# Batch 7's k and v loads, v casts and k exponential at other places of a hand-ordered attention-then-MLP kernel

## The chip, the core and the metric

The kernel runs on one core of a Trainium2 chip. The time is that of one execution on the device in microseconds (us). Before the change it is 277.86 us, the median of three runs (277.82 to 278.19).

## The reference

Attention without a score matrix, for 8 batches of 8 heads, 576 positions and 64 columns, and behind it two matrix products:

```python
def _attn_ref(q, k, v):
    q_s = np.exp(q - np.max(q, axis=-1, keepdims=True))
    q_s = q_s / (np.sum(q_s, axis=-1, keepdims=True) + 1e-09)
    k_s = np.exp(k - np.max(k, axis=2, keepdims=True))
    k_s = k_s / (np.sum(k_s, axis=2, keepdims=True) + 1e-09)
    kv = np.einsum('bhsd,bhse->bhde', k_s, v)
    return np.einsum('bhsd,bhde->bhse', q_s, kv)

def _moe_ref(x, w_in, w_out):
    h = x @ w_in
    return np.maximum(0.01 * h, h) @ w_out
```

q is normalized over its 64 columns, k over the 576 positions. The result, with batch and position joined to 4608 tokens of 512 columns, is x; `w_in` is 512x2048 and `w_out` 2048x512.

## The kernel before

The 4608 tokens are worked through in 9 tiles of 512, counted from 0. A tile has 64 matmuls of layer 1 (16 blocks j of hidden columns, 4 matmuls each, line L563), whose sums ScalarE passes through the leaky activation (`leaky`, L572), and then layer 2 (L584): four sub-blocks of 128 tokens, each of 16 matmuls into one PSUM buffer `pout`. Tiles 3 and 4, of which the change speaks, both go so. At the end of a sub-block ScalarE copies `pout` to `out_sb` (`store`, L578) and SyncE issues two stores of 128 KB (L581). There are two `pout` buffers for layer 2, so sub-block 3 writes into the one that sub-block 1's copy has to have read; there are four `out_sb`.

The attention of later batches runs beside that. For one batch the steps are:

- `load_all` (L84): SyncE loads k, q and v into buffers of a pool of six (`raw_pool`). A buffer comes free when the last reader of its old tile is done. Batch 7's k takes the place of batch 5's v, batch 7's v that of batch 5's k, and batch 7's q that of batch 5's q.
- k: VectorE takes the maximum over positions (`k_max`, that is `k_tree`, L160), carries it across partitions and subtracts it (`k_less`, that is `k_allmax` and `k_sub`, L167 to L198); ScalarE takes the exponential (`k_exp`, L206).
- v: two casts to bf16 into `vb2` (`v_cast`, L216), on ScalarE for batches 5 to 7 (`casts_act`).
- q: maximum and difference on VectorE (`q_front`, L245 and L304), the exponential on ScalarE (`q_exp`, L312), sum, reciprocal and product on VectorE (`q_ready`, L321, L323 and L328), and a transposing DMA that SyncE issues (`q_turn`, L551).
- `attend_kv(b)`: on TensorE, the k-v product of batch b+1 (L341, into `pokv`) interleaved with the product of batch b's q and its k-v matrix (L479); on VectorE the scaling of the new k-v matrix (`kd_make`, L361 and L362); on ScalarE six copies into `xT`, the input of layer 1 (`x_keep`, L500).

The order is written out by hand. `at(t, u, ...)` hangs steps on a place of tile t: u from 0 to 15 is behind layer 1's block u, u = 16+4s+m behind the 4(m+1)-th matmul of sub-block s. The steps of a place are recorded when TensorE's program gets there, and each engine then takes its own instructions in that order, without overtaking. So a step moved by `at` moves on every engine that it uses, SyncE's queue of DMA issues among them, and an instruction that waits holds up all behind it on its engine. Every DMA of SyncE takes the next of eight semaphores in turn and first waits until the DMA that had that semaphore before has landed.

Two steps behind these matter as well. At (5, 12), `in_weight_sums` gives GpSimd eight sums and differences of `w_in` halves (L824). It takes inputs that were there long before, and writes into `t`, whose buffer is that of batch 7's v: GpSimd, which has nothing ahead of it, starts when batch 7's v casts have read that buffer. And at (5, 0) and (5, 9) batch 7's q exponential and its transpose follow.

Of the kernel before, what the change touches and what calls it, by code (L numbers as in the profile page):

```python
# [26 lines left out]
def kernel(  # L27
# [50 lines left out]
    def load(src, b, name, cuts, t=None):  # L78
        t = raw(name) if t is None else t
        flat = src[b].rearrange("h s d -> (h s d)").rearrange(  # L80
            "(hl p r d) -> p hl r d", hl=HL, p=P, r=R
        )
        for hs, rs in cuts:
            nc.sync.dma_start(  # L84
                out=t[:, hs, rs].rearrange("p h r d -> p h (r d)"),
                in_=flat[:, hs, rs].rearrange("p h r d -> p h (r d)"),
            )
        return t

    ALLH, ALLR = slice(0, HL), slice(0, R)  # L90
# [114 lines left out]
    def k_exp(b, hs):  # L205
        nc.scalar.activation(  # L206
            out=st[b]["ke"][:, :, hs].rearrange("p r h d -> p h r d"),
            in_=st[b]["k"][:, hs],
            func=AF.Exp,
        )  # L210

    def v_cast(eng, b, gg):
        o = vb2[b % 2][:, :, gg, :, 0:D].rearrange("p r h d -> p h r d")
        i = st[b]["v"][:, 2 * gg : 2 * gg + 2]
        if eng is nc.scalar:
            eng.copy(out=o, in_=i)  # L216
        else:
            eng.tensor_copy(out=o, in_=i)  # L218
# [10 lines left out]
    def turned(name):  # L229
        return qT_pool.tile([P, XE.stop, P], BF16, name=name, tag="qT")  # L230
# [87 lines left out]
    def q_sum(b, rs, hs=ALLH):  # L318
        n, m = rs.stop - rs.start, hs.stop - hs.start
        qsum = small_pool.tile([P, n, HL], FP32, name="qsum")[:, :, 0:m]  # L320
        nc.vector.reduce_sum(out=qsum, in_=q_cols(b, rs, hs), axis=AX.X)  # L321
        st[b]["qrec", rs.start, hs.start] = qrec = small_pool.tile([P, n, HL], FP32, name="qrec")[:, :, 0:m]
        nc.vector.reciprocal(out=qrec, in_=qsum)  # L323

    def q_norm(b, rs, hs=ALLH, out=None):
        n, m = rs.stop - rs.start, hs.stop - hs.start
        qes = q_cols(b, rs, hs)
        nc.vector.tensor_tensor(  # L328
            out=qes if out is None else out,
            in0=qes,  # L330
            in1=st[b]["qrec", rs.start, hs.start].unsqueeze(3).to_broadcast([P, n, m, D]),
            op=ALU.mult,
        )


    def kv_quads(b, gg, outs, rs=ALLR):
        for r in range(R)[rs]:
            for hp in range(2):
                for hh in range(2):
                    rows = slice(hh * L, (hh + 1) * L)  # L340
                    nc.tensor.matmul(  # L341
                        outs[hh][hp * D : (hp + 1) * D, 0 : D + 1],
                        lhsT=st[b]["ke"][rows, r, 2 * gg + hp],
                        rhs=vb2[b % 2][rows, r, gg, hp, 0 : D + 1],
                        start=(r == 0),
                        stop=(r == R - 1),
                    )
# [9 lines left out]
    def kd_make(b):  # L357
        for hh in range(2):
            pkv = st[b]["pkv"][hh]
            krec = small_pool.tile([P, 2, 1], FP32, name="krec")  # L360
            nc.vector.reciprocal(out=krec, in_=pkv[:, :, D : D + 1])  # L361
            nc.vector.tensor_tensor(  # L362
                out=kd2[b % 2][:, :, hh],
                in0=pkv[:, :, 0:D],
                in1=krec.to_broadcast([P, 2, D]),
                op=ALU.mult,
            )
# [96 lines left out]
    def cross(b, gg, outs, rows):  # L464
        for hp in range(2):
            for hh in range(2):
                half = slice(hp * D, (hp + 1) * D)
                ls = slice(hh * L, (hh + 1) * L)
                if b == 0 and rows.start == R3.start:
                    rhs = st[1]["X1"][:, X8][:, gg : gg + 1, ls]  # L470
                elif b == 1 and rows.start == RE.start:
                    rhs = st[1]["X1"][:, XE].rearrange("c (r g) l -> c g r l", g=2)[:, gg, :, ls]
                elif b == 1:
                    rhs = st[1]["X1"][:, XH[gg], ls]
                elif "qX" in st[b]:
                    rhs = st[b]["qX"].rearrange("c (r g) (h l) -> c g h r l", g=2, h=2)[:, gg, hh, rows]
                else:
                    rhs = st[b]["qT"][:, 2 * hh + gg, rows]
                nc.tensor.matmul(  # L479
                    outs[hp][hh * D : (hh + 1) * D].rearrange("p (r l) -> p r l", l=L),  # L480
                    lhsT=kd0[half, gg, hh, hp] if b == 0 else kd2[b % 2][half, gg, hh],
                    rhs=rhs[half],
                    start=True,
                    stop=True,
                )

    def attend(b, ggs, rows, pool=psB_pool, tag=BANK_TAG):
        n = (rows.stop - rows.start) * L
        ps = [pool.tile([P, len(ggs), n], FP32, name="po", tag=tag) for _ in range(2)]
        for i, gg in enumerate(ggs):  # L490
            cross(b, gg, [ps[hp][:, i] for hp in range(2)], rows)
        st[b]["po", ggs, rows.start] = ps

    def x_keep(eng, b, ggs, rows, hp):
        ps = st[b]["po", ggs, rows.start][hp]
        c0, c1 = b * S + rows.start * L, b * S + rows.stop * L
        s0 = 2 * ggs[0] + hp
        o = xT[:, s0 : 2 * ggs[-1] + hp + 1 : 2, c0:c1]
        if eng is nc.scalar:
            eng.copy(out=o, in_=ps)  # L500
        else:
            eng.tensor_copy(out=o, in_=ps)

    def attend_kv(b, rows=R7, rest=RE):
        n = 2 * (rest.stop - rest.start) * L
        both = [psB_pool.tile([P, n + 2 * (D + 2)], FP32, name="pokv", tag=BANK_TAG) for _ in range(2)]
        ps = [a[:, 0:n].rearrange("p (g c) -> p g c", g=2) for a in both]
        st[b + 1]["pkv"] = pkv = [a[:, n:].rearrange("p (g d) -> p g d", g=2) for a in both]
        part = lambda gg, r0, r1: kv_quads(b + 1, gg, [pkv[hh][:, gg] for hh in range(2)], slice(r0, r1))
        part(0, 0, 6)  # L510
        attend(b, (0,), rows)
        part(0, 6, R)
        part(1, 0, 3)
        attend(b, (1,), rows)
        part(1, 3, R)
        for gg in range(2):
            cross(b, gg, [ps[hp][:, gg] for hp in range(2)], rest)
        keep = [lambda gg=gg, hp=hp: x_keep(nc.scalar, b, (gg,), rows, hp) for gg in range(2) for hp in range(2)]
        st[b]["po", (0, 1), rest.start] = ps
        kd_make(b + 1)  # L520
        for fn in keep:
            fn()
        for hp in range(2):
            x_keep(nc.scalar, b, (0, 1), rest, hp)
# [23 lines left out]
    def q_turn(b, rs=ALLR):  # L548
        if rs.start == 0:
            st[b]["qX"] = turned("qX")[:, 0 : 2 * R]  # L550
        nc.sync.dma_start_transpose(  # L551
            out=st[b]["qX"][:, 2 * rs.start : 2 * rs.stop],
            in_=st[b]["qe"][:, rs].rearrange("p r h d -> p (r h d)"),
        )
# [40 lines left out]
    def at(t, u, *fns):  # L595
        while t > 0 and u >= 32:
            t, u = t + 1, u - 32
        hooks.setdefault((t, u), []).extend(fns)
# [7 lines left out]
    def load_all(b, order="kqv"):  # L606
        for name in order:
            cuts = [(H0, ALLR), (H1, ALLR)] if b == B - 1 or (b, name) in ((B - 2, "q"), (B - 2, "v")) else [(ALLH, ALLR)]
            st[b][name] = load(dict(q=q, k=k, v=v)[name], b, f"{name}_raw", cuts)
# [155 lines left out]
    def k_max(b, t, u):  # L765
        at(t, u, lambda: k_begin(b), lambda: q_begin(b), lambda: k_tree(b, ALLH))

    def k_less(b, t, u):
        at(t, u, lambda: k_allmax(b), lambda: k_sub(nc.vector, b, ALLH))

    def q_ready(b, t, u):
        at(t, u, lambda: q_sum(b, ALLR), lambda: q_norm(b, ALLR))

    def casts_act(b, *slots):
        for gg, (t, u) in enumerate(slots):
            at(t, u, lambda gg=gg: v_cast(nc.scalar, b, gg))
# [12 lines left out]
    at(3, 20, lambda: q_exp(5, ALLR))  # L789
    q_ready(5, 3, 20)  # L790
    casts_act(6, (3, 28), (3, 30))
    at(3, 31, lambda: q_turn(5), lambda: load_all(7, "kvq"))
    k_less(6, 3, 31)
    at(4, 4, lambda: k_exp(6, ALLH))
    q_front(6, 4, 4)
    at(4, 9, lambda: q_exp(6, ALLR))
    k_max(7, 4, 9)
    q_ready(6, 4, 9)
    at(4, 17, lambda: attend_kv(5))
    k_less(7, 4, 18)  # L800
    at(4, 20, lambda: q_turn(6))
    casts_act(7, (4, 20), (4, 22))
    at(4, 24, lambda: k_exp(7, ALLH))
    q_front(7, 4, 24)
    at(4, 28, lambda: attend_kv(6))
    at(5, 0, lambda: q_exp(7, ALLR))
# [712 lines left out]
```

## Time and profile before

| what | value |
|---|---|
| median of three runs | 277.86 us (277.82 to 278.19) |
| the profiled execution, its own time | 277.69 us |
| span of its instructions | 275.7 us |
| TensorE, busy | 269.0 us, 98% |
| VectorE, busy | 225.9 us, 82% |
| ScalarE, busy | 184.9 us, 67% |
| GpSimd, busy | 81.8 us, 30% |
| tile 3, layer 1 and layer 2 | about 105.5 to 119.2 and 119.2 to 134.3 us |
| tile 4, layer 1 and layer 2 | about 134.3 to 148.1 and 148.1 to 165.3 us |

All times inside the program are counted from the span's start. In the profile's lines PE is TensorE, PEld its weight loads, DVE VectorE, ACT ScalarE, POOL GpSimd, and SPq SyncE's queue of DMA issues. `ke<-k_raw` means that `ke` is written and `k_raw` read. In a timeline a line has the start, the length, the engine, the code line, the operation, the tiles and how many instructions it merges; `[0.75 <-ACT ke L206]` says that the engine stood idle for 0.75 us ahead of it, and what ended that.

### The profile page before, as it was taken

How to read it: one execution, taken by the hardware profiler on the slowest of the kernel's cores; microseconds unless marked ns; L12 is line 12 of the kernel's file. 1: busy time of each engine (PE TensorE's matmuls, PEld its weight loads, DVE VectorE, ACT ScalarE, POOL GpSimd, SP SyncE). 2: the span in 40 equal slices, each digit the busy share in tenths (PEclk: the TensorE clock that was granted, in tenths of full speed). 3: DMA queues.
4: the chain of work that ended last, by engine and by line, in shares of the span. 5: the costliest groups of instructions: out<-in, count | busy, mean ns of one | idle time of the engine just before them, and what ended most of it. 6: DMA issues, size and time to landing. Idle time of an engine off the chain costs nothing.

```text
span 275.7 us, 5464 instructions
## 1 busy us (share of the span) xinstructions
PE 269.0 (98%) x2114; PEld 162.9 (59%) x2114; DVE 225.9 (82%) x330; ACT 184.9 (67%) x336; POOL 81.8 (30%) x97
## 2 busy tenths in 40 slices
PE   8899999999999999999999989999999999999994
PEld 3478644444444454454444444466776777889994
DVE  2996995899999999978978998979954756669962
ACT  4977573784489368985797669657746767984241
POOL 2866460149003000000000194000001999950000
PEclk9999999999999999999999999999999999999999
DMA  7999999987997699696398271400033000015254
GB/s 246 332 209 322 242 267 262 391 272 238 251 386 259 70 348 333 110 390 186 83 268 326 56 148 38 86 4 0 2 76 76 0 4 0 0 36 131 66 115 115
DMA packets 40569, 46.48 MB, mean 169 GB/s; under 512 B 18912, under 2 KB 24288, under 8 KB 40544
## 3 DMA queue, kind: packets, MB, share of 16 engines
q1 hardware_dynamic: 36720, 41.56, 51.3%
q0 software_dynamic: 3504, 4.20, 8.7%
q10 hardware_dynamic: 320, 0.39, 0.4%
q8 instruction: 16, 0.26, 0.4%
q14 instruction: 9, 0.07, 0.1%
HBM read 36.70 MB, written 9.44 MB: 167 GB/s over the span
## 4 chain that ended last, share of the span: by engine, by line
PE 85%; DVE 8%; DMA 4%; ACT 1%; SPq 1%; issue 0%; DVEq 0%
PE ph L563 32%; PE pout L584 21%; PE pout L1094 10%; PE pq L1343 10%; PE pp L1062 9%; DMA k_raw<-in_k_dram 4%; DVE t L160 2%; PE po L479 1%; ACT ke L206 1%; DVE k_raw L198 1%; DVE qe L328 1%; DVE qsum L321 1%; PE pkv L341 1%; PE pokv L341 1%; PE pkv L419 0%; DVE k_raw L410 0%
## 5 line engine op out<-in xcount | busy, mean ns | idle before, releaser
L563 PE MATMUL ph<-xT,w_in_sb 128*128 128x512 bf16 (+1 forms) x512 | 99.5, 353 | 0.0
L563 PEld LDWEIGHTS <-w_in_sb 128*128 128x128 bf16 x512 | 49.4, 98 | 46.0 <-issue 0.2
L584 PE MATMUL pout<-w_out_sb,gj 128*128 128x512 bf16 x320 | 71.4, 379 | 0.0
L572 ACT ACTIVATE gj<-ph 128x512 bf16<-128x512 f32 x88 | 49.1, 605 | 13.7 <-PE ph L563 13.1
L584 PEld LDWEIGHTS <-gj 128*128 128x128 bf16 x320 | 30.6, 98 | 36.1 <-issue 0.2
L824 POOL TENSOR_TENSOR t<-w_in_sb 128x256 fp32r<-128x256 bf16 x16 | 12.3, 772 | 68.7 <-DMA out_dram<-out_sb 68.7
L328 DVE TENSOR_TENSOR qe<-qe,qrec 128x2304 bf16<-128x2304 bf16 (+5 forms) x13 | 21.5, 1657 | 0.4
L321 DVE TENSOR_REDUCE qsum<-qe 128x36 f32<-128x2304 bf16 (+5 forms) x13 | 20.1, 1542 | 2.2 <-ACT qe L312 2.0
L206 ACT ACTIVATE ke<-k_raw 128x2304 bf16<-128x2304 f32 (+2 forms) x13 | 18.0, 1383 | 4.2 <-DVE k_raw L198 3.7
L578 ACT COPY out_sb<-pout 128x512 f32<-128x512 f32 x16 | 9.4, 589 | 16.5 <-PE pout L584 13.4
L245 DVE TENSOR_REDUCE qmax<-q_raw 128x36 f32<-128x2304 f32 (+5 forms) x13 | 20.0, 1537 | 0.5 <-DMA q_raw<-in_q_dram 0.5
L312 ACT ACTIVATE qe<-q_raw 128x2304 bf16<-128x2304 f32 (+5 forms) x13 | 17.3, 1328 | 4.2 <-POOL q_raw L304 3.2
L198 DVE TENSOR_TENSOR k_raw<-k_raw,kall 128x1152 f32<-128x1152 f32 (+2 forms) x10 | 18.1, 1821 | 0.3
L572 ACT ACTIVATE xT<-ph 128x512 bf16<-128x512 f32 x24 | 13.9, 605 | 5.9 <-PE ph L563 5.8
L304 POOL TENSOR_TENSOR q_raw<-q_raw,qmax 128x512 f32<-128x512 f32 (+3 forms) x7 | 11.8, 1681 | 20.4 <-DVE qmax L245 20.0
L1259 DVE COPY u<-pp 128x512 f32<-128x512 f32 x8 | 5.5, 692 | 13.6 <-PE pp L1062 13.6
L500 ACT CAST xT<-po 128x448 bf16<-128x448 f32 (+3 forms) x31 | 13.2, 509 | 4.4 <-PE po L479 4.4
L824 POOL TENSOR_TENSOR t<-w_in_sb,t 128x256 fp32r<-128x256 bf16 x16 | 15.1, 943 | 0.6
L218 POOL CAST vb<-v_raw 128x1152 bf16<-128x1152 f32 x7 | 9.8, 1436 | 17.1 <-DMA v_raw<-in_v_dram 17.1
L304 DVE TENSOR_TENSOR q_raw<-q_raw,qmax 128x2304 f32<-128x2304 f32 (+1 forms) x6 | 13.7, 2290 | 0.2
L1062 PE MATMUL pp<-s,t 128*128 128x512 f32 x48 | 13.9, 398 | 0.0
L160 DVE TENSOR_TENSOR t<-k_raw 128x512 f32<-128x512 f32 (+1 forms) x11 | 10.2, 930 | 3.7 <-DMA k_raw<-in_k_dram 3.6
(169 smaller groups left out, 434.0 us busy)
## 6 DMA issues: line engine op xcount, KB each, us to landing
out_dram<-out_sb SPq DMA_DIRECT2D x60, 128.0 KB, 2.5
k_raw<-in_k_dram SPq DMA_DIRECT2D x8, 576.0 KB, 5.8
v_raw<-in_v_dram SPq DMA_DIRECT2D x8, 576.0 KB, 7.4
q_raw<-in_q_dram SPq DMA_DIRECT2D x4, 1152.0 KB, 9.4
v_raw<-in_v_dram SPq DMA_DIRECT2D x4, 1152.0 KB, 11.6
k_raw<-in_k_dram SPq DMA_DIRECT2D x4, 1152.0 KB, 6.3
q_raw<-in_q_dram SPq DMA_DIRECT2D x4, 576.0 KB, 8.5
w_in_sb<-in_moe_w_in_dram POOLq DMA_DIRECT2D x7, 256.0 KB, 6.9
```

The source lines that it names most:

```text
L198: eng.tensor_tensor(out=ks, in0=ks, in1=st[b]["kall"][:, hs].unsqueeze(2).to_broadcast([P, n, R, D]), op=ALU.subtract,)
L206: nc.scalar.activation(out=st[b]["ke"][:, :, hs].rearrange("p r h d -> p h r d"), in_=st[b]["k"][:, hs], func=AF.Exp,)
L304: eng.tensor_tensor(out=qs, in0=qs, in1=st[b]["qmax", rs.start, hs.start].unsqueeze(3).to_broadcast([P, m, n, D]), op=ALU.subtract,)
L321: nc.vector.reduce_sum(out=qsum, in_=q_cols(b, rs, hs), axis=AX.X)
L328: nc.vector.tensor_tensor(out=qes if out is None else out, in0=qes, in1=st[b]["qrec", rs.start, hs.start].unsqueeze(3).to_broadcast([P, n, ...
L563: nc.tensor.matmul(ph, lhsT=w_in_sb[:, cb, j * P : (j + 1) * P], rhs=xT[:, cb, c0 : c0 + n], start=(cb == 0 and first), stop=(cb == NB - 1 ...
L572: nc.scalar.activation(out=o, in_=ph, func=AF.Prelu, alpha=LEAKY_SLOPE)
L584: nc.tensor.matmul(pout, lhsT=g_sb[j // 2][:, j % 2, tsub * P : (tsub + 1) * P], rhs=w_out_sb[:, j, os], start=(j == 0), stop=(j == NF - 1),)
L824: eng.tensor_tensor(out=late[o], in0=a, in1=b, op=ALU.subtract)
L1062: nc.tensor.matmul(ps, lhsT=w(c), rhs=a(c), start=(first and c == 0), stop=(c == 1), skip_group_check=True)
L1094: nc.tensor.matmul(ps[:, i], lhsT=a(m)[:, i * P : (i + 1) * P], rhs=w(m), start=(first and m == 0 and i == 0), stop=(m == NH - 1 and i == ...
L1343: nc.tensor.matmul(ps[i], lhsT=a(m)[:, i * P : (i + 1) * P], rhs=w(m), start=(first and m == 0 and (each or i == 0)), stop=(m == NH - 1 an ...
```

## The change

```diff
     q_ready(5, 3, 20)
     casts_act(6, (3, 28), (3, 30))
-    at(3, 31, lambda: q_turn(5), lambda: load_all(7, "kvq"))
+    at(3, 22, lambda: load_all(7, "kv"))
+    at(3, 31, lambda: q_turn(5), lambda: load_all(7, "q"))
     k_less(6, 3, 31)
...
     q_ready(6, 4, 9)
+    casts_act(7, (4, 16), (4, 16))
     at(4, 17, lambda: attend_kv(5))
     k_less(7, 4, 18)
-    at(4, 20, lambda: q_turn(6))
-    casts_act(7, (4, 20), (4, 22))
-    at(4, 24, lambda: k_exp(7, ALLH))
+    at(4, 18, lambda: q_turn(6))
+    at(4, 22, lambda: k_exp(7, ALLH))
     q_front(7, 4, 24)
```

Four steps move: batch 7's k and v loads from the end of tile 3 to its sub-block 1, batch 7's v casts from sub-block 1 of tile 4 to the start of its sub-block 0, batch 6's q transpose from sub-block 1 to sub-block 0, and batch 7's k exponential from sub-block 2 to sub-block 1. No instruction is added or taken away, and each of batch 7's three tiles takes the same buffer as before. TensorE's, VectorE's and GpSimd's orders stay as they were; lines behind the change have numbers higher by one.

SyncE's queue, from tile 3's output stores to batch 7's q transpose, before:

```order
L581 DMA out_dram<-out_sb 64x512 x8
L551 DMA_TRANSPOSE qX<-qe 128x18x128
L84 DMA k_raw<-in_k_dram 128x2x576 x2
L84 DMA v_raw<-in_v_dram 128x2x576 x2
L84 DMA q_raw<-in_q_dram 128x2x576 x2
L581 DMA out_dram<-out_sb 64x512 x2
L551 DMA_TRANSPOSE qX<-qe 128x18x128
L581 DMA out_dram<-out_sb 64x512 x6
```

The same stretch of SyncE's queue with the change:

```order
L581 DMA out_dram<-out_sb 64x512 x2
L84 DMA k_raw<-in_k_dram 128x2x576 x2
L84 DMA v_raw<-in_v_dram 128x2x576 x2
L581 DMA out_dram<-out_sb 64x512 x6
L551 DMA_TRANSPOSE qX<-qe 128x18x128
L84 DMA q_raw<-in_q_dram 128x2x576 x2
L551 DMA_TRANSPOSE qX<-qe 128x18x128
L581 DMA out_dram<-out_sb 64x512 x8
```

Batch 7's k and v loads now stand behind tile 3's first two stores instead of behind its eighth and batch 5's transpose; batch 6's transpose (the second) stands ahead of all of tile 4's stores instead of behind two of them.

ScalarE, from tile 4's last six layer-1 activations on, as the difference (`vb_134` and `ke` are batch 7's, `out_sb` the copies of tile 4's sub-blocks, `xT` the copies of `attend_kv(5)` and then of `attend_kv(6)`):

```order
 L572 ACTIVATE gj<-ph 128x512 x6
+L216 COPY vb_134<-v_raw 128x2x9x64 x2
 L500 COPY xT<-po 128x448 x4
 L500 COPY xT<-pokv 128x2x128 x2
 L578 COPY out_sb<-pout 128x512
-L216 COPY vb_134<-v_raw 128x2x9x64 x2
-L578 COPY out_sb<-pout 128x512
 L206 ACTIVATE ke<-k_raw 128x4x9x64
-L578 COPY out_sb<-pout 128x512
+L578 COPY out_sb<-pout 128x512 x2
 L500 COPY xT<-po 128x448 x4
```

The two v casts move ahead of `attend_kv(5)`'s copies, and the k exponential now stands between the output copies of sub-blocks 0 and 1, where it stood between those of 1 and 2.

## The prediction

> **What bounds the kernel now.** I read the waits of TensorE first, then the chain of waits, then the timelines of the engines between 138 and 170 us. Two rows of the page and one of the view of TensorE's waits:
>
> ```profile
> PE 269.0 (98%) x2114; PEld 162.9 (59%) x2114; DVE 225.9 (82%) x330; ACT 184.9 (67%) x336; POOL 81.8 (30%) x97
> PEclk9999999999999999999999999999999999999999
> PE pokv L341 <- ACT ke L206: 0.8, 1, 0.8
> ```
>
> TensorE is busy for 98% of the span at full clock, and the third row is its only wait behind the first 16 us. So a change in the middle of the program is worth what it does to TensorE's idle time, and nothing else. That one wait is the target. The chain of waits (start, length, what) shows who makes it:
>
> ```profile
> 139.80 5.44 DMA k_raw<-in_k_dram
> 145.33 1.24 DVE t L160
> 156.74 2.57 DVE k_raw L198
> 159.34 2.13 ACT ke L206
> 161.51 0.38 PE pokv L341 x24
> ```
>
> Batch 7's k lands at 145.24; VectorE takes its maximum (`k_tree(7)`), then works on batch 6's q, then subtracts batch 7's maximum (L198); ScalarE takes the exponential (L206, `k_exp(7)`), and TensorE's k-v product of batch 7 (L341, inside `attend_kv(6)`) waits for it. How long it really waits, from TensorE's timeline (start, length, instruction, count):
>
> ```profile
> 148.08 1.89 PE L584 MATMUL pout<-w_out_sb,gj 128*128 128x512 bf16 x8
> 149.90 0.38 PE L341 MATMUL pokv<-vb,ke 64*64 64x65 bf16 x24
> 151.09 9.67 PE L584 MATMUL pout<-w_out_sb,gj 128*128 128x512 bf16 x44
> 161.51 0.38 PE L341 MATMUL pokv<-vb,ke 64*64 64x65 bf16 x24 [0.75 <-ACT ke L206]
> 165.32 0.38 PE L563 MATMUL ph<-xT,w_in_sb 128*128 128x512 bf16 x1
> ```
>
> One 128x512 matmul lasts 0.38 (last row), so the 8 of the first row start up to 148.08+1.89-0.38 = 149.59, and the unhindered step from there to the k-v product is 149.90-149.59 = 0.31. The 44 start up to 151.09+9.67-0.38 = 160.38; unhindered, the product of batch 7 would start at 160.69. It starts at 161.51: **0.82 us are lost**, and that is the most that the change can win. The 44 start (9.67-0.38)/43 = 0.216 apart; 8 of them end sub-block 0 of the tile, 16 each are sub-blocks 1 and 2, so sub-block 3 starts with the 41st, at 151.09+40x0.216 = 159.73.
>
> **The change, part by part.** VectorE's rows:
>
> ```profile
> 140.20 2.56 DVE L304 TENSOR_TENSOR q_raw<-q_raw,qmax 128x2304 f32<-128x2304 f32 x1
> 145.33 1.23 DVE L160 TENSOR_TENSOR t<-k_raw 128x1024 f32<-128x1024 f32 x1 [2.56 <-DMA k_raw<-in_k_dram]
> 147.77 0.43 DVE L160 TENSOR_TENSOR kmax<-t,k_raw 128x256 f32<-128x256 f32 x1
> 148.12 2.55 DVE L321 TENSOR_REDUCE qsum<-qe 128x36 f32<-128x2304 bf16 x1
> 151.11 2.56 DVE L328 TENSOR_TENSOR qe<-qe,qrec 128x2304 bf16<-128x2304 bf16 x1
> 156.74 2.56 DVE L198 TENSOR_TENSOR k_raw<-k_raw,kall 128x2304 f32<-128x2304 f32 x1
> 161.80 3.08 DVE L304 TENSOR_TENSOR q_raw<-q_raw,qmax 128x2304 f32<-128x2304 f32 x1
> 169.18 2.55 DVE L321 TENSOR_REDUCE qsum<-qe 128x36 f32<-128x2304 bf16 x1 [0.99 <-ACT qe L312]
> ```
>
> And ScalarE's:
>
> ```profile
> 143.74 2.16 ACT L312 ACTIVATE qe<-q_raw 128x2304 bf16<-128x2304 f32 x1
> 145.75 3.13 ACT L572 ACTIVATE gj<-ph 128x512 bf16<-128x512 f32 x6
> 150.51 1.84 ACT L500 CAST xT<-po 128x448 bf16<-128x448 f32 x4 [1.63 <-PE po L479]
> 155.31 2.21 ACT L216 CAST vb<-v_raw 128x1152 bf16<-128x1152 f32 x2
> 157.42 0.59 ACT L578 COPY out_sb<-pout 128x512 f32<-128x512 f32 x1
> 159.34 2.12 ACT L206 ACTIVATE ke<-k_raw 128x2304 bf16<-128x2304 f32 x1 [1.32 <-DVE k_raw L198]
> 161.37 0.57 ACT L578 COPY out_sb<-pout 128x512 f32<-128x512 f32 x1
> 167.01 2.14 ACT L312 ACTIVATE qe<-q_raw 128x2304 bf16<-128x2304 f32 x1
> ```
>
> *k and v loads earlier.* SyncE's queue before, then the landing times of k's loads and of the q transposes (issues from 110 to 190 us):
>
> ```profile
> 125.36 10.87 SPq L581 DMA_DIRECT2D out_dram<-out_sb  x8
> 136.34 2.78 SPq L551 DMA_TRANSPOSE qX<-qe  x1
> 139.16 1.11 SPq L84 DMA_DIRECT2D k_raw<-in_k_dram  x2
> 156.68 2.89 SPq L551 DMA_TRANSPOSE qX<-qe  x1
> 174.89 2.69 SPq L551 DMA_TRANSPOSE qX<-qe  x1
> ...
> DMA to landing us min/median/max: 4.6/5.4/6.2
> ...
> DMA to landing us min/median/max: 4.5/4.7/5.3
> ```
>
> Tile 3's eight output stores start at 125.36; the loads now follow the first two. The two halves of k are issued at about 127 and, at up to 6.2 us, land by about 134, against 145.24. Their buffers were read last by batch 5's v casts and k exponential, long done. The other six stores, q's load and the transpose of batch 5's q queue behind four loads more; the six stores feed nobody soon, and that transpose, issued at 136.34, is used behind the product at 149.90. Earlier loads cost nothing while they are under 10 us late.
>
> With k there, `k_tree(7)` starts when VectorE is free, 140.20+2.56 = 142.76 instead of 145.33, and ends 2.56 earlier, at 145.7. The next step, batch 6's sum, needs ScalarE's exponential: 143.74+2.16 = 145.90, plus the 0.03 that the same pair takes for batch 7 (167.01+2.14 = 169.15 to 169.18): 145.93 instead of 148.12. **VectorE gains 2.19, not 2.56**: the wait on the load gives way to one on ScalarE. Behind it follows the same sequence, so L198 starts at 156.74-2.19 = 154.55 and ends at 157.11.
>
> *Casts of v earlier.* Two casts (2.21) go from behind the first output copy to behind the last layer-1 activation. ScalarE stood idle there for 1.63 us, so the four copies of `xT` end 0.4 later, at 152.7; nobody waits for them before tile 5. The first output copy still comes earlier, near 153.3, because the `pokv` casts ahead of it waited for VectorE.
>
> *k exponential earlier.* It starts 0.03 after L198, at 157.15, and ends 2.12 later, at 159.27 (161.46 before). TensorE takes it up 0.05 later (161.46 to 161.51): 159.32, well under 160.69. The 0.82 goes. **But the exponential now stands ahead of the copy of sub-block 1**, and sub-block 3 writes to that copy's PSUM buffer (there are two). The copy ran at 157.42 to 158.01, off the path; now it starts 0.09 before the exponential ends (161.46 against 161.37), lasts 0.59 and is over at 159.77; with 0.05 to TensorE, sub-block 3 starts at 159.82 instead of 159.73. **A new wait of 0.09.**
>
> *Transpose of batch 6's q earlier.* It needs VectorE's L328, then over at 151.48, and goes ahead of the first pair of stores: issued at about 151.5, landed by about 156.5 at 4.5 to 5.3 us, needed behind the product at 160.69. Those stores go at 154.4, no later than before.
>
> *What is late next.* Later steps move with TensorE: batch 7's q exponential follows the same activation, and its transpose, issued at 174.89 and landed by 180.2 at the latest, moves by about as much. It is needed here:
>
> ```profile
> 180.19 0.68 PE L479 MATMUL po<-qX,kd 64*64 64x448 bf16 x16
> ```
>
> At the median of 4.7 it lands at 179.6; even if it stayed while TensorE came 0.73 earlier (179.46), the loss would be some 0.1.
>
> *GpSimd, which no line of the diff names.* Its first work on layer 1's weight sums writes into the buffer of batch 7's v, so it starts when the casts end: at 151.05 instead of 157.60. Before:
>
> ```profile
> 157.60 2.23 POOL L824 TENSOR_TENSOR t<-w_in_sb 128x256 fp32r<-128x256 bf16 x1 [68.74 <-DMA out_dram<-out_sb]
> 161.80 0.67 POOL L824 TENSOR_TENSOR t<-w_in_sb 128x256 fp32r<-128x256 bf16 x1
> ```
>
> One such sum takes 0.67, but 2.23 beside L198: it ended 0.53 behind L198's end (159.83 against 159.30). In the other direction, VectorE's L304 took 3.08 instead of 2.56 when a sum (161.80 to 162.47) started with it: 0.52 more, which is all but the last 0.15 of the sum. So these operations exclude each other. Now the first sum meets L328 and ends 0.53 behind it, at 152.01; the second to fifth end at 154.65 (2.64 on, as 159.83 to 162.47), against L198's start at 154.55: 0.10 of overlap, under that 0.15, so no delay; the sixth waits. The bounds are 0 and 0.52 (L304's row); I take 0, with little room.
>
> The Trainium skill, page "SBUF — State Buffer", section "SBUF: two separate sides", says that a VectorE operation with two SBUF inputs and a GpSimd operation that reads SBUF hold one port pair in turn, each for its whole length. The rows agree except for that 0.15; taken to the letter, the sum would lose 0.10 more.
>
> **Sum**: 0.82-0.09 = 0.73 faster. The profiled execution took 277.69 (275.7 of span and 1.99 around it): 276.96. The median of the three runs shown, 277.86, lies 0.17 above it: on that scale 277.13.
>
> **Rivals.**
> 1. *GpSimd delays L198.* A sum that starts just ahead of L198 holds it for up to 0.52; the exponential, the copy and sub-block 3 slip as much, and the new wait becomes up to 0.61. Gain 0.21 at worst: 277.65. For it: 0.05 us of room. Against it: both sides start from L328's end, so they move together.
> 2. *The new wait outweighs the old one* (slower). If VectorE gains only G, sub-block 3 starts at 162.01-G (161.46-G, less 0.09, plus 0.59 and 0.05), a wait of 2.28-G for the 0.82 removed: the kernel is slower once G falls under 1.46, up to 1.46 slower at G = 0, 279.3; with two operations held instead of one (G = 1.15), 278.2. Place: sub-block 3's first matmul. For it: the order on ScalarE is fixed, and nothing overtakes the exponential. Against it: it takes 0.73 more than I count on VectorE.
> 3. *The loads do not come early.* If k lands later than 143.8, G is under 1.46 again: 277.9 to 279.3. They would have to land 10 us behind my count.
>
> **How the numbers follow.** Forecast 0.60 (276.9 to 277.3), rival 1 0.20 (277.3 to 277.65), rival 2 0.15, rival 3 0.05. The predicted time is the forecast's, 277.1. The range runs from the whole 0.82 on the profiled execution, 276.9, less 0.1 of scatter, to rival 1's end plus 0.2 (the profiled execution and the median lie 0.17 apart), 277.9. About 0.2% (0.56 us) is what a measurement of this kernel can tell from no change. The forecast lies beyond it: faster 0.60. Rival 1, and the parts of 2 and 3 near balance: same 0.24. The rest: slower 0.16.
>
> **What would show it.** In the changed kernel's profile the row L341 <- ACT ke is gone from TensorE's waits, and at most some 0.1 us at L584, released by the copy at L578, stands there. VectorE's 2.56 of idle time behind the load is gone, a short one behind ScalarE's L312 follows, and L198 starts near 154.6 and lasts 2.56. GpSimd starts near 151. Wrong I am if L198 lasts 3 us (rival 1), if the wait at L584 is over 0.8 (rival 2), or if VectorE still waits for k (rival 3).

## The result and the profile after

| | median, us | runs | ratio to before on the same chip, 95% interval |
|---|---|---|---|
| before | 278.19 (277.82 to 278.84) | 7 | |
| the change | 277.16 (276.94 to 277.34) | 7 | 0.9961 (0.9949 to 0.9973) |

The change is faster by 1.03 us at the medians; by the ratio, 0.27% to 0.51%. The profiled execution of the changed kernel took 277.08 (before 277.69), its span 275.0 (275.7).

TensorE's busy row and its clock row on the page of the changed kernel; 24 of its 2114 matmul records are missing there, which is why its busy time seems lower than before:

```profile
PE 266.7 (97%) x2090; PEld 162.8 (59%) x2114; DVE 225.1 (82%) x330; ACT 184.5 (67%) x336; POOL 78.6 (29%) x97
PEclk9999999999999999999999999999999999999999
```

TensorE's waits in the changed kernel (releaser, total, times, longest):

```profile
PE pout L373 <- POOL zero L103: 1.0, 1, 1.0
PE kT L384 <- POOL gate L619: 0.8, 1, 0.8
PE pout L584 <- issue: 0.8, 5, 0.2
PE kallp L399 <- DVE kr L394: 0.6, 2, 0.3
PE pkv L419 <- ACT ke L206: 0.2, 1, 0.2
```

The row of L341 behind `ke` is gone. The first two and the last two rows belong to the start of the program; the third is the gaps that missing records leave, 0.16 at a time. The chain of waits between 125 and 165 us, which held `DMA k_raw`, three VectorE steps and `ke` before, is TensorE's own work now:

```profile
by line: PE pout L584 58.6%; PE ph L563 34.9%; PE pokv L341 3.5%; PE po L479 1.9%; issue 1.1%; PE pokv L479 0.6%
```

TensorE's timeline, the rows that answer to those shown of before:

```profile
148.17 1.89 PE L584 MATMUL pout<-w_out_sb,gj 128*128 128x512 bf16 x8
149.99 0.38 PE L341 MATMUL pokv<-vb,ke 64*64 64x65 bf16 x24
151.41 9.51 PE L584 MATMUL pout<-w_out_sb,gj 128*128 128x512 bf16 x43 [0.16 <-issue]
160.84 0.38 PE L341 MATMUL pokv<-vb,ke 64*64 64x65 bf16 x24
```

I call the time from the start of tile 4's layer 2 to batch 7's k-v product the **stretch**. It took 161.51-148.08 = 13.43 before and takes 160.84-148.17 = 12.67 now. Everything ahead of it is the same work (it starts 0.09 later in this execution), and everything behind it takes the same time: from the k-v product to the end of the own time it is 277.69-161.51 = 116.18 before and 277.08-160.84 = 116.24 now. So the stretch holds the whole effect, 0.76 us between these two executions. VectorE's timeline in the changed kernel:

```profile
142.77 1.22 DVE L160 TENSOR_TENSOR t<-k_raw 128x1024 f32<-128x1024 f32 x1
146.01 2.55 DVE L321 TENSOR_REDUCE qsum<-qe 128x36 f32<-128x2304 bf16 x1 [0.39 <-ACT qe L312]
149.01 2.56 DVE L328 TENSOR_TENSOR qe<-qe,qrec 128x2304 bf16<-128x2304 bf16 x1
154.65 2.56 DVE L198 TENSOR_TENSOR k_raw<-k_raw,kall 128x2304 f32<-128x2304 f32 x1
159.70 2.56 DVE L304 TENSOR_TENSOR q_raw<-q_raw,qmax 128x2304 f32<-128x2304 f32 x1
```

ScalarE's timeline in the changed kernel:

```profile
148.86 2.20 ACT L216 CAST vb<-v_raw 128x1152 bf16<-128x1152 f32 x2
153.18 0.65 ACT L578 COPY out_sb<-pout 128x512 f32<-128x512 f32 x1
157.24 2.12 ACT L206 ACTIVATE ke<-k_raw 128x2304 bf16<-128x2304 f32 x1 [3.41 <-DVE k_raw L198]
159.27 0.57 ACT L578 COPY out_sb<-pout 128x512 f32<-128x512 f32 x1
160.07 0.58 ACT L578 COPY out_sb<-pout 128x512 f32<-128x512 f32 x1 [0.23 <-ACT out_sb L578]
```

VectorE no longer waits for `k_raw` (no bracket at L160); it waits 0.39 for ScalarE's L312 instead, and L198 starts at 154.65 (156.74 before). ScalarE's exponential ends at 159.36, ahead of the 160.78 at which TensorE takes it up unhindered (12.61 behind the start of the stretch, as the kernels without any wait below show). SyncE's queue in the changed kernel:

```profile
127.31 1.13 SPq L84 DMA_DIRECT2D k_raw<-in_k_dram  x2
129.77 6.91 SPq L581 DMA_DIRECT2D out_dram<-out_sb  x6
136.80 3.29 SPq L551 DMA_TRANSPOSE qX<-qe  x1
151.72 2.94 SPq L551 DMA_TRANSPOSE qX<-qe  x1
```

And its GpSimd, the first, the fifth and the sixth sum:

```profile
151.14 0.96 POOL L825 TENSOR_TENSOR t<-w_in_sb 128x256 fp32r<-128x256 bf16 x1 [62.05 <-ACT vb L216]
154.06 0.67 POOL L825 TENSOR_TENSOR t<-w_in_sb 128x256 fp32r<-128x256 bf16 x1
154.80 2.93 POOL L825 TENSOR_TENSOR t<-w_in_sb,t 128x256 fp32r<-128x256 bf16 x1
```

The row of k's two loads among the DMA issues (KB each, median time from issue to landing):

```profile
k_raw<-in_k_dram SPq DMA_DIRECT2D x2, 576.0 KB, 4.8
```

The k loads are issued at 127.3 and 127.9 (139.2 and 139.8 before) and take 4.3 and 5.2 to land, so the two halves are there at 131.6 and 133.1, 9.7 us ahead of use. GpSimd starts when the second cast of v ends.

What stayed open after this pair of traces: the medians differ by 1.03, the two stretches by 0.76.

### The profile page after: what moved, and what is told of

Same layout as the page of the kernel before. It is cut to its first block, busy times and chain, and to the rows that moved or that the text cites. A ratio compares the mean times of both kernels' runs of the same rounds, so it can differ in the third digit from the quotient of the medians.

```text
span 275.0 us, 5446 instructions
## 1 busy us (share of the span) xinstructions
PE 266.7 (97%) x2090; PEld 162.8 (59%) x2114; DVE 225.1 (82%) x330; ACT 184.5 (67%) x336; POOL 78.6 (29%) x97
## 4 chain that ended last, share of the span: by engine, by line
PE 93%; DVE 3%; DMA 2%; issue 1%; ACT 0%; SPq 0%
PE ph L563 35%; PE pout L584 25%; PE pout L1095 10%; PE pq L1344 10%; PE pp L1063 9%; DMA k_raw<-in_k_dram 2%; PE po L479 2%; DVE t L160 1%; PE pokv L341 1%; PE pkv L341 1%; PE pkv L419 0%; DVE k_raw L410 0%; ACT ke L206 0%; DVE kmax L160 0%; DVE kd L434 0%
## 5 line engine op out<-in xcount | busy, mean ns | idle before, releaser
L584 PE MATMUL pout<-w_out_sb,gj 128*128 128x512 bf16 x309 | 70.1, 379 | 1.1 <-issue 0.8
L825 POOL TENSOR_TENSOR t<-w_in_sb 128x256 fp32r<-128x256 bf16 x16 | 11.1, 693 | 62.1 <-ACT vb L216 62.1
L328 DVE TENSOR_TENSOR qe<-qe,qrec 128x2304 bf16<-128x2304 bf16 (+5 forms) x13 | 21.5, 1656 | 0.4
L312 ACT ACTIVATE qe<-q_raw 128x2304 bf16<-128x2304 f32 (+5 forms) x13 | 17.2, 1326 | 4.2 <-POOL q_raw L304 3.2
L198 DVE TENSOR_TENSOR k_raw<-k_raw,kall 128x1152 f32<-128x1152 f32 (+2 forms) x10 | 18.0, 1820 | 0.3
L825 POOL TENSOR_TENSOR t<-w_in_sb,t 128x256 fp32r<-128x256 bf16 x16 | 13.1, 818 | 0.6
```

Of the source, the lines that this page charges most:

```text
L198: eng.tensor_tensor(out=ks, in0=ks, in1=st[b]["kall"][:, hs].unsqueeze(2).to_broadcast([P, n, R, D]), op=ALU.subtract,)
L328: nc.vector.tensor_tensor(out=qes if out is None else out, in0=qes, in1=st[b]["qrec", rs.start, hs.start].unsqueeze(3).to_broadcast([P, n, ...
L584: nc.tensor.matmul(pout, lhsT=g_sb[j // 2][:, j % 2, tsub * P : (tsub + 1) * P], rhs=w_out_sb[:, j, os], start=(j == 0), stop=(j == NF - 1),)
L825: eng.tensor_tensor(out=late[o], in0=a, in1=b, op=ALU.subtract)
```

## The experiments

All times in this table are of profiled executions. The wait is TensorE's idle time in the stretch, but for the three small ones that are explained below; "behind" is the own time less the start of batch 7's k-v product. What a kernel loses in the stretch is its length less the 12.61 of the kernels without any wait. At full clock that is 0.07 more than the idle time that the profile shows at the k-v product, and 0.16 more at a sub-block, since a matmul's shown length, 0.38, reaches beyond the unhindered step to the next one (0.31 to the k-v product, 0.216 inside layer 2).

| kernel | own time | stretch starts | stretch | wait in it | behind |
|---|---|---|---|---|---|
| before | 277.69 | 148.08 | 13.43 | 0.75 at the k-v product | 116.18 |
| before, 2nd (r1_before) | 280.35 | 150.20 | 13.91 | 1.23 at the k-v product | 116.24 |
| before, 3rd (r2_before) | 278.24 | 148.06 | 13.98 | 1.29 at the k-v product | 116.20 |
| the change | 277.08 | 148.17 | 12.67 | 0.06 at sub-block 3 | 116.24 |
| the change, 2nd (r3_after) | 277.02 | 148.06 | 12.69 | 0.07 at sub-block 3 | 116.27 |
| loads alone (e1_loads_only) | 276.82 | 148.09 | 12.61 | none | 116.12 |
| order alone (e2_order_only) | 281.17 | 148.14 | 16.09 | 2.55 at sub-block 3 | 116.94 |
| order alone, 2nd (r5_order_only) | 279.48 | 148.00 | 15.32 | 2.55 at sub-block 3 | 116.16 |
| order alone, 3rd (r6_order_only) | 281.02 | 148.07 | 16.16 | 2.55 at sub-block 3 | 116.79 |
| k exponential back (e3_exp_back) | 276.83 | 148.02 | 12.61 | none | 116.20 |
| the same, 2nd (r4_exp_back) | 277.03 | 148.14 | 12.61 | none | 116.28 |
| GpSimd shifted (e4_pool_shift) | 277.28 | 147.95 | 13.00 | 0.39 at sub-block 3 | 116.33 |
| q loaded first (e5_q_first) | 280.93 | 148.48 | 16.27 | 1.94 at sub-block 2, 1.50 at the k-v product | 116.18 |
| casts alone (e6_casts_only) | 278.55 | 148.34 | 13.99 | 1.31 at the k-v product | 116.22 |

The waits of 0.06, 0.07 and 0.39 are steps between matmuls: sub-block 3's first one comes 0.280 and 0.288 after its forerunner in the two executions of the change, and 0.610 in e4_pool_shift, where 0.216 is the unhindered step.

### The loads alone: e1_loads_only

```
-    at(3, 31, lambda: q_turn(5), lambda: load_all(7, "kvq"))
+    at(3, 22, lambda: load_all(7, "kv"))
+    at(3, 31, lambda: q_turn(5), lambda: load_all(7, "q"))
```

> The kernel before with one edit: batch 7's k and v loads behind tile 3's first two stores. ScalarE's order and the q transpose stay as before. Theory (the load alone held TensorE up): VectorE's subtraction (L198) ends at about 157.1, the k exponential, behind the copy of sub-block 1, at about 159.3, and TensorE's 0.82 us at the k-v product is gone with no new wait: 0.82 faster than before, that is 0.06 faster than the whole change, and no gap at sub-block 3. GpSimd starts near 155.7 instead of 151.1. Rival (the moved casts, exponential and transpose are needed too): a part of the 0.82 stays at the k-v product, or at the q product behind it, and the time lies between before and the whole change.

Measured: 276.87 (276.82 to 276.96, 6 runs) against 277.96 of before on that chip, ratio 0.9957 (0.9942 to 0.9972). TensorE's timeline at both ends of the stretch:

```profile
148.09 1.89 PE L584 MATMUL pout<-w_out_sb,gj 128*128 128x512 bf16 x8
160.70 0.38 PE L341 MATMUL pokv<-vb,ke 64*64 64x65 bf16 x24
```

ScalarE's exponential in the same kernel, which stands at its old place:

```profile
157.16 2.12 ACT L206 ACTIVATE ke<-k_raw 128x2304 bf16<-128x2304 f32 x1
```

The loads alone bring the whole gain. The exponential follows VectorE's L198 at once without being moved, because the copy of sub-block 1 ahead of it is over by then.

### ScalarE's order alone, three executions: e2_order_only, r5_order_only, r6_order_only

```
+    casts_act(7, (4, 16), (4, 16))
-    at(4, 20, lambda: q_turn(6))
-    casts_act(7, (4, 20), (4, 22))
-    at(4, 24, lambda: k_exp(7, ALLH))
+    at(4, 18, lambda: q_turn(6))
+    at(4, 22, lambda: k_exp(7, ALLH))
```

> The change without the earlier loads: casts, q transpose and k exponential moved, loads where they were before. Theory (the exponential holds up the copy of sub-block 1): k still lands near 145.2, the exponential still ends near 161.5, the copy behind it near 162.0, and sub-block 3, due at 159.73, waits 2.28 us: 1.46 slower than before. GpSimd, started at 151.05 by the early casts, gets its first sum in ahead of VectorE's L328 (due at 151.11) and delays it by up to 0.5: then 1.9 slower, near 279.8 against 277.9. Rival (the order on ScalarE does not matter while the exponential's own end stays): no slower than before.

Measured: 280.47 (279.53 to 281.55, 4 runs) against 277.96, ratio 1.0087 (1.0058 to 1.0117). ScalarE's timeline in e2_order_only:

```profile
159.86 2.13 ACT L206 ACTIVATE ke<-k_raw 128x2304 bf16<-128x2304 f32 x1 [3.91 <-DVE k_raw L198]
161.89 1.05 ACT L578 COPY out_sb<-pout 128x512 f32<-128x512 f32 x2
```

TensorE's in the same kernel:

```profile
162.51 1.79 PE L584 MATMUL pout<-w_out_sb,gj 128*128 128x512 bf16 x4 [2.55 <-ACT out_sb L578]
164.23 0.55 PE L341 MATMUL pokv<-vb,ke 64*64 64x65 bf16 x24
```

This is the slower side that the prediction described: with late loads the exponential is late, the copy of sub-block 1 queues behind it, and sub-block 3 waits 2.55 us. But the four times fell into two pairs, 279.53 and 279.76, near the 279.8 that was expected, and 281.17 and 281.55; and the profiled execution, of the upper pair, has something more: four matmuls take 1.79 behind the wait, where four take 1.02 elsewhere. Two more executions were taken to see what parts the pairs.

> The late-load kernel of e2_order_only again. Its four times lay in two pairs, 279.53 and 279.76 with a granted clock of 1.000, 281.17 and 281.55 with 0.993. The profiled one was of the upper pair: after the wait of 2.55 us at the third output sub-block, the matmuls from 162.5 to 166.0 ran at a granted clock of 0.50 to 0.58, where the same ones of before run at 1.00. Theory (the pairs differ by that stretch alone): if this execution is of the lower pair, its time is 279.5 to 279.8, the wait is still 2.0 to 2.7 and no stretch behind it has a clock below 0.9; if it is of the upper pair it looks like the first. Rival (the pairs differ by the length of the wait): in the lower pair the wait is about 1 us.

> The same kernel once more, to have one execution of each pair if the two fall evenly: the same two expectations, 279.5 to 279.8 with the wait but no slow stretch, or 281.2 to 281.6 with both.

Measured: 279.48 and 281.02, one of each. The table by stretches of time (busy time of PE, PEld, DVE, ACT, POOL with counts, then granted clock, DMA share, GB/s) for r5_order_only:

```profile
162.50:164.20 1.70, 1.70 (x75) 0.96 (x76) 1.70 (x1) 0.57 (x2) 0.00 (x0) 1.00 0.41 90
164.20:166.20 2.00, 1.84 (x43) 1.03 (x37) 1.93 (x6) 2.00 (x6) 0.00 (x0) 1.00 0.86 185
```

The same two stretches of time in e2_order_only:

```profile
162.50:164.20 1.70, 1.69 (x4) 0.40 (x3) 1.70 (x1) 0.44 (x1) 0.00 (x0) 0.53 0.34 73
164.20:166.20 2.00, 2.00 (x89) 1.51 (x88) 0.68 (x1) 1.02 (x3) 0.00 (x0) 0.54 0.90 200
```

And r5_order_only's TensorE:

```profile
162.36 1.02 PE L584 MATMUL pout<-w_out_sb,gj 128*128 128x512 bf16 x4 [2.55 <-ACT out_sb L578]
163.32 0.38 PE L341 MATMUL pokv<-vb,ke 64*64 64x65 bf16 x24
```

The wait is the same 2.55 in both, so the rival (a shorter wait in the lower pair) falls. The difference is the clock: in e2_order_only it is 0.53 and 0.54 for the 3.7 us behind the wait, in r5_order_only 1.00. That costs 16.09-15.32 = 0.77 in the stretch and 116.94-116.16 = 0.78 behind it. The third execution repeats the first (clock 0.50 and 0.63 in the same two rows). So the order alone costs 279.48-277.69 = 1.79 through the wait (k landed at the same place in these two traces: L160 starts 2.74 and 2.75 ahead of the stretch), and in three of six executions 1.5 more through the clock: in the traces of e2_order_only and r6_order_only, and by its mean clock of 0.994 in the other time of the upper pair, which has no trace.

That the wait is 2.55 each time is not because k landed at one time: L160 starts 2.49, 2.74 and 2.53 ahead of the stretch in the three. The early casts let GpSimd's first sum start 2.97 behind the start of the stretch, just ahead of VectorE's L328, which then takes 2.76, 3.01 and 2.81 instead of 2.56 and ends 6.05 to 6.06 behind the start of the stretch in all three. Here GpSimd and not the landing of k sets when VectorE goes on (point 7 below).

### The k exponential back, the rest as in the change: e3_exp_back, r4_exp_back, r3_after

```
-    at(4, 22, lambda: k_exp(7, ALLH))
+    at(4, 24, lambda: k_exp(7, ALLH))
```

> The change with the k exponential back behind the copy of sub-block 1. Theory: the gap of 0.06 at sub-block 3's first matmul goes, the k-v product starts without a wait, 0.82 faster than before and 0.06 faster than the change, seen in the trace and not in the times. Rival (that gap is no wait on the copy): the gap of 0.06 stays.

Measured: 276.81 (276.51 to 276.89, 6 runs), ratio 0.9954 (0.9939 to 0.9968) to the same 277.96. TensorE at both ends of the stretch:

```profile
148.02 1.89 PE L584 MATMUL pout<-w_out_sb,gj 128*128 128x512 bf16 x8
160.63 0.38 PE L341 MATMUL pokv<-vb,ke 64*64 64x65 bf16 x24
```

12.61, as with the loads alone: the new wait is gone, and nothing is lost by it. By the medians this kernel lay 0.35 below the change, by the stretches 0.06; the two times came from two chips. Both kernels were run again side by side.

> The change, unchanged, beside the change with k exponential back at its old place (r4_exp_back) on one chip. Its first time was 277.16 on another chip, and that of the kernel with k exponential back was 276.81: 0.35 apart, where the trace shows a new wait of 0.064 only (the step from one matmul of the third sub-block to the next is 0.280 instead of 0.216). Theory (the new wait is small, the rest is the difference of two chips): 276.9 here, within 0.15 of r4_exp_back. Rival (moving k exponential up costs 0.3 more than its wait shows): 277.15, and 0.25 to 0.45 above r4_exp_back.

> The change with batch 7's k exponential back at tile 4's slot 24, so that no output copy stands behind it. Theory: 276.8, within 0.15 of the change on this chip. Rival: 276.8, and 0.25 to 0.45 below the change.

Measured on one chip, against 278.24 of before: the change 277.02 (276.66 to 277.22, 5 runs), ratio 0.9964 (0.9950 to 0.9978); with the exponential back 276.92 (276.56 to 277.28, 6 runs), ratio 0.9961 (0.9946 to 0.9975). They are 0.10 apart, well inside either's scatter, and the stretches are again 12.69 and 12.61. So few times could not exclude the lower end of the rival's 0.25 to 0.45; the traces speak against it, since behind the stretch they differ by 0.01 only (116.27 and 116.28). The move of the exponential costs the 0.06 to 0.08 of its wait and gains nothing.

### GpSimd shifted by one short operation: e4_pool_shift

The change, with one more subtraction of 128x128 elements at the start of GpSimd's weight sums; its result is read by nothing.

```
+        if i == 0:
+            nc.gpsimd.tensor_tensor(
+                out=late["t"][:, 0:2, 512:576], in0=w_in_sb[:, 0:2, 0:64], in1=w_in_sb[:, 0:2, 64:128], op=ALU.subtract
+            )
```

> The change with one more GpSimd operation ahead of its first weight sum (128x128 elements, written to an unused part of the sums' tile), so that its sums run some 0.44 later against VectorE. Theory (a GpSimd sum and a VectorE operation with two inputs in SBUF exclude each other): a sum now starts just ahead of L198, L198 lasts 2.85 to 3.05 instead of 2.56, the exponential and the copy of sub-block 1 slip by 0.3 to 0.5, and so does sub-block 3: 0.3 to 0.5 slower than the change. Rival (they only slow each other when VectorE's operation is the first): L198 lasts 2.56 and the time is that of the change.

Measured: 277.28 (276.98 to 278.18, 10 runs), ratio 0.9975 (0.9962 to 0.9988). VectorE's L198 in this kernel:

```profile
154.43 2.89 DVE L198 TENSOR_TENSOR k_raw<-k_raw,kall 128x2304 f32<-128x2304 f32 x1
```

GpSimd's sum that runs into it:

```profile
154.24 0.66 POOL L825 TENSOR_TENSOR t<-w_in_sb 128x256 fp32r<-128x256 bf16 x1
```

TensorE's sub-block 3:

```profile
160.00 1.02 PE L584 MATMUL pout<-w_out_sb,gj 128*128 128x512 bf16 x4 [0.23 <-ACT out_sb L578]
```

The sum ends at 154.90, 0.47 behind L198's start, and L198 takes 2.89 instead of 2.56. The 0.33 appears in full at sub-block 3: its wait grows from 0.06 to 0.39, the stretch from 12.67 to 13.00. This is the prediction's first rival, forced; the mechanism is real, and the change stays clear of it by 0.03 to 0.06 us of overlap (point 7 below). The trace carries this; by the ratios to before, 0.9975 beside the change's 0.9961 on another chip, the intervals overlap.

### Why the medians differ by more than the traces: r1_before, r2_before

The kernel before, unchanged, profiled twice more.

> The kernel before, unchanged, for a second profiled execution. What is to be explained: the change gained 1.03 us by the medians (interval 0.75 to 1.42), but TensorE's trace of one execution each shows 0.76. Theory (the landing of batch 7's k varies): in the first profiled execution the maximum of k_raw (L160) started at 145.33, the wait at the k-v product was 0.75 and the own time 277.69, so 276.94 without the wait. In this execution the wait should be the start of L160 less 144.58, within 0.1, and the own time less the wait 276.9, within 0.15: an execution of 278.2 has a wait of about 1.25 and starts L160 at 145.85. Rival (the scatter lies elsewhere, in the start or the end): the wait stays at 0.75 within 0.1 and the own time moves without it.

> The kernel before once more, for a third profiled execution, with the same two expectations: by the landing theory the own time less the wait at the k-v product of batch 7 is 276.9 within 0.15 whatever the own time is, and the wait follows the start of the maximum of k_raw one for one; by the rival the wait is 0.75 in every execution.

Measured: 280.35 and 278.24. In r2_before, the transfer of k's second half on the chain of waits (start, length):

```profile
139.75 6.02 DMA k_raw<-in_k_dram
```

VectorE's maximum in the same execution:

```profile
145.86 1.23 DVE L160 TENSOR_TENSOR t<-k_raw 128x1024 f32<-128x1024 f32 x1 [3.11 <-DMA k_raw<-in_k_dram]
```

And TensorE's k-v product:

```profile
162.04 0.38 PE L341 MATMUL pokv<-vb,ke 64*64 64x65 bf16 x24 [1.29 <-ACT ke L206]
```

The transfer took 6.02 where it took 5.44 in the first execution, at nearly the same issue time (139.10 and 139.16); L160 starts at 145.86, 0.53 later, and the wait is 1.29, 0.54 longer. The expected wait was 145.86-144.58 = 1.28, and the own time less the wait is 276.95, against 276.94. In r1_before the own time less the wait is 279.12, off the expected 276.9: TensorE waited 1.7 for a block of layer 1's weights, which no other execution did for more than 0.2, and its stretch starts 2.1 later. Measured from the start of the stretch it agrees: L160 starts 147.93-150.20 = -2.27 from it, 0.48 later than in the first execution (145.33-148.08 = -2.75), and the wait is 0.48 longer. The rival (a constant wait) falls. The first profiled execution, at 277.69, was one of before's shorter ones; by the same subtraction, which is an estimate, a median of 278.0 to 278.2 stands for a wait of 1.1 to 1.3.

### The landing 3 us later: e5_q_first

```
-    at(3, 31, lambda: q_turn(5), lambda: load_all(7, "kvq"))
+    at(3, 31, lambda: q_turn(5), lambda: load_all(7, "qkv"))
```

> Before with batch 7's late loads issued in the order q, k, v instead of k, v, q, so that k lands about 3.0 us later (each half took 1.5 us behind the one ahead of it: 143.72, 145.23, 146.74, 148.24). Nothing else moves. Theory (the landing of k ends the chain to the k-v product): the wait there grows from 0.75 by about 2.9 to some 3.7 us, and the time by as much, to 280.8 to 281.1; as a wait of 2.55 us was followed in e2_order_only by matmuls at half the granted clock, up to 1.7 more, 282.7. Rival (VectorE has slack that takes the delay, or v's landing bounds the batch): less than 1.5 more, below 279.7.

Measured: 280.88 (280.64 to 281.23, 4 runs) against 278.15, ratio 1.0096 (1.0079 to 1.0112). VectorE's maximum in this kernel:

```profile
148.63 1.23 DVE L160 TENSOR_TENSOR t<-k_raw 128x1024 f32<-128x1024 f32 x1 [5.47 <-DMA k_raw<-in_k_dram]
```

ScalarE's casts ahead of the copy of sub-block 0:

```profile
157.47 0.77 ACT L500 CAST xT<-pokv 128x256 bf16<-128x256 f32 x2 [4.72 <-DVE krec L361]
```

TensorE's two waits in the stretch (total, times, longest):

```profile
PE pout L584 <- ACT out_sb L578: 1.9, 1, 1.9
PE pokv L341 <- ACT ke L206: 1.5, 1, 1.5
```

Counted from the start of the stretch, L160 starts 2.90 later than in the first execution of before, and the stretch is 2.84 longer: the landing is paid almost one for one, and VectorE has no slack. The place was expected wrongly: 1.94 of it is lost already at sub-block 2, whose output buffer waits for the copy of sub-block 0, and that copy stands on ScalarE behind casts that wait for VectorE. The half clock that I allowed for did not follow these two shorter waits in this trace: the granted clock is 1.00 in the rows behind both.

### The casts alone: e6_casts_only

```
+    casts_act(7, (4, 16), (4, 16))
-    at(4, 20, lambda: q_turn(6))
-    casts_act(7, (4, 20), (4, 22))
+    at(4, 18, lambda: q_turn(6))
```

> Before with the casts of v and the transpose of batch 6's q moved up, but the k and v loads left late and k exponential left at tile 4's slot 24. It parts the two moves in ScalarE's order that made the late-load kernel (e2_order_only) 2.5 us slower. Theory (that loss is the output copy behind the late k exponential, and nothing else): no copy stands behind it here, the only wait is that at the k-v product as before, and the time is that of before, 277.9 to 278.5 on this chip with a few tenths for GpSimd's earlier start (the normalization L328 lasted 2.76 instead of 2.56 in e2_order_only); ratio 0.999 to 1.003. Rival (the earlier casts carry it): a ratio of 1.006 or more.

Measured: 278.20 (277.81 to 278.73, 12 runs) against 278.15, ratio 1.0002 (0.9992 to 1.0012). TensorE's k-v product of batch 7:

```profile
162.33 0.38 PE L341 MATMUL pokv<-vb,ke 64*64 64x65 bf16 x24 [1.31 <-ACT ke L206]
```

The wait is where and what it is in r2_before. So moving the casts and the transpose is worth nothing measurable by itself, and the wait at sub-block 3 in e2_order_only comes with the exponential ahead of the copy, which is all that the two kernels differ in. The casts still have a part in that wait's length: the 0.20 to 0.45 that GpSimd takes from L328 there. In this trace k landed later (L160 starts 2.20 ahead of the stretch), the sum and L328 met for 0.06 only, and nothing was lost.

## Why the prediction was right

The forecast was 277.1, and 277.16 and 277.02 were measured on two chips. By its own steps:

1. *TensorE's wait at the k-v product is the target.* Right: the stretch holds the whole effect in every kernel run, and what lies behind takes 116.1 to 116.3 wherever the clock stayed up. **The size was off.** The 0.82 came from one execution; the profile's row for it, 0.75, read 1.23 and 1.29 in two others, since it contains the transfer of k (5.44 to 6.02). This is the term that was mis-sized: in a typical execution about 1.2 of wait goes, not 0.75. The predicted time still fits, because a kernel without the wait does not inherit its scatter; the predicted gain, 0.73, was too small beside 1.03 and 1.22 (278.24-277.02) on the two chips. How closely 277.13 fits is partly luck: the 0.17 added to come from the profiled execution to the median was, if the account above holds, scatter of that same wait, which the change takes away. Without it the sum says 276.96, and the two medians lie 0.06 and 0.20 above that.
2. *Loads early.* Right, with its replacement: k landed by 133.1, VectorE waits 0.39 for ScalarE, and L198 comes 156.74-154.65 = 2.09 earlier, 2.18 with the start of the stretch taken off (predicted 2.19).
3. *Casts early.* Right: the first output copy at 153.18 (predicted near 153.3), and nothing gained or lost (e6_casts_only).
4. *k exponential early.* It ends at 159.36 and the wait goes, as predicted, and the new wait at sub-block 3 is 0.064 (predicted 0.09). But the step credits the move with what the loads alone do: e1_loads_only and e3_exp_back lose the wait with the exponential at its old place. The move brings only the new wait.
5. *Transpose of batch 6's q.* Right: issued at 151.72 (predicted 151.5), landed by 156.3, needed behind the product at 160.84.
6. *What is late next.* Nothing was: the time behind the k-v product is unchanged.
7. *GpSimd.* Right, and the room was as small as stated: the fifth sum ends at 154.73, 0.08 behind L198's start, and L198 takes 2.56; in r3_after the overlap is 0.11, and L198 takes 2.56 again. Such a meeting with a long overlap, in r5_order_only:

```profile
150.97 0.67 POOL L824 TENSOR_TENSOR t<-w_in_sb 128x256 fp32r<-128x256 bf16 x1 [62.28 <-ACT vb L216]
151.04 3.01 DVE L328 TENSOR_TENSOR qe<-qe,qrec 128x2304 bf16<-128x2304 bf16 x1
```

The sum ends 0.60 behind L328's start, and L328 takes 0.45 more than its 2.56. In the other traces 0.06 to 0.11 cost nothing (L328 in e6_casts_only, L198 in the two executions of the change), 0.35 costs 0.20 (L328 in e2_order_only), 0.39 costs 0.25 (L328 in r6_order_only), 0.47 costs 0.33 (L198 in e4_pool_shift). It is the overlap less about 0.14. The Trainium skill's rule (page "SBUF — State Buffer", section "SBUF: two separate sides") taken to the letter, the whole overlap, is too strict for these records by that 0.14. Whether GpSimd lets go early or its records end late is not shown.

Of the rivals, the first happens with one short GpSimd operation more (e4_pool_shift); the second is what the kernel does without the early loads: for G = 0 a wait of 2.28 was worked out, GpSimd takes 0.45 more from L328, together 2.73, and r5_order_only loses 15.32-12.61 = 2.71. The clock the prediction did not have. The third did not happen.

Two kernels here are no slower than the change: the loads alone, and the change with the exponential back. Their stretch is 0.06 to 0.08 shorter in every trace. The timings, 276.92 beside 277.02 on one chip, cannot tell them from the change. What makes the transfer of k take between 5.44 and 6.02 in the kernel before stays open; nothing was run on it.

## What to carry to other kernels

A wait that has a DMA's landing in its chain is not one number: profile the kernel more than once before pricing its removal, and count the time of the kernel without it, which scatters less (on one chip 277.32 to 278.76 before, 276.82 to 276.96 with the loads alone), as the firmer forecast. When several steps are moved together, ask of each whether it still does anything once the others are in place: here the loads did all, and a move in an in-order queue added a small wait, which was 2.55 us in the kernel whose loads came late. Give the shared engine (here ScalarE) the operation that frees a buffer before one that waits, unless the wait is surely over.

## What the runs showed of the hardware

**Half the clock behind a wait of 2.55 us.** In e2_order_only and r6_order_only the granted clock was 0.50 to 0.63 in the two rows behind the wait, in r5_order_only 1.00 after the same wait, and the two waits of 1.94 and 1.50 in e5_q_first's trace were followed by no such drop. From rows of 0.2 us I estimate that the clock fell at 162.6 in e2_order_only, 0.1 after TensorE had gone on, and at 162.3 in r6_order_only, 0.2 before it went on, and that it was 0.50 for about 3.4 us in both. The Trainium skill, page "TensorE: Matmul & The Clock Gate", section "What's actually happening", says that the clock halves after at least one idle window of some 3.4 us, and that the window runs free and does not start anew with a kernel. That half the executions drop after the same wait, and at different places beside it, fits free-running windows; that 2.55 us of idleness suffice speaks against a whole window being needed. No run here tells what share of a window does it.
